# Gate and up of a bilinear GLU as 2x2 blocks with Strassen's seven products, down following per pair of segments

## The chip, the cores and the metric

One core of one Trainium2 chip runs the whole kernel in one launch. The metric is device time in microseconds (us), the median of three runs. The engines are called PE (matrix products), DVE (vector), ACT (scalar functions), POOL (general SIMD) and SP (which only issues DMA transfers here). Each runs its own queue in order and waits on semaphores for the others.

## The reference

A transformer block on x of 2048 rows and 512 columns, modulated by a vector c: attention with a compressive memory over four segments of 512 rows, and then a bilinear gated linear unit.

```python
h = layernorm(x) * (1 + ca) + sa
x = x + ga * A(h)            # 32 heads of 16, 4 segments of 512 rows, each with causal softmax
                             # attention and a memory of the segments before it; then @ wo
h = layernorm(x) * (1 + cb) + sb
x = x + gb * ((h @ w_gate) * (h @ w_up)) @ w_down      # w_gate, w_up: 512 x 1376, w_down: 1376 x 512
```

All is float32. Each large product is made in three matmuls of rounded operands: an operand is split into a rounded high part (`hi`, `H`) and the rest (`lo`, `L`), and high x high, low x high and high x low are summed.

## The kernel before

The four segments of 512 rows (`s`, `L` = 512) go through the attention as 32 units of four heads each, software-pipelined. While PE, DVE, ACT and POOL work on a unit, two generators, `fill_a` and `fill_b`, are advanced step by step to put other work between: `fill_a` the layer norm and the projections of the next segment, `fill_b` the product with wo (`wo_mm`), the layer norm of segment 0 for the GLU (`lnC(0)`) and the preparation of the first two tiles of GLU weights (`prep(0)`, `prep(1)`). Segment 3's product with wo (`ps3`, `wo_row`, `wo_add`) comes after the last unit. Its result rows, x1, go to DRAM (`x1d`).

Then the GLU stage runs by segment. F = 1376 is cut into eleven tiles (`ft`: ten of 128, one of 96; NF = 11). For a tile `i`, `gate_up(i)` makes gate and up (two PSUM banks, 12 matmuls each: 4 blocks of the contraction by 3 parts, each 128 x 128 weights against 512 columns of the transposed, normalised segment `chH`/`chL`). ACT copies the gate out (`gs`), DVE multiplies with up, ACT and DVE split the product (`mH`, `mL`), and 12 matmuls with w_down (`dH`, `dL`) add to four accumulators `acc`, one for each 128 rows. The order is written out:

```python
gate_up(0)
for i in range(NF):
    if i + 1 < NF:
        gate_up(i + 1)
    ...            # 12 matmuls of tile i into acc
```

so that a tile's down stands behind the next tile's gate and up. During segment 0 `prep(i + 1)` brings the weights of the coming tile: gate, up and down by DMA, split by DVE, ACT and POOL, the down rows multiplied by `gbb` (the modulation gb) on DVE. All eleven tiles then stay in SBUF for the other segments. The layer norm of segment s + 1 (`lnC(s + 1)`, a call of `ln`: statistics and normalisation on DVE, 16 transposes on PE in four groups `ctp`, ACT scaling, a split) is made in the middle of segment s. At a segment's end the rows of x1 come back (`xc`), DVE adds `acc`, and the sum is stored.

The program is ordered by a scheduler that keeps each engine's instructions mostly as written and hands out buffers as they come free. Two helpers tie things: `MM` and `TP` chain each PE instruction to the one before, and `pin(i)` orders an instruction behind the last such PE instruction when the schedule is made, without a wait on the chip. `last_pe[0] = None` takes that tie away; the GLU stage before calls `nc.tensor.matmul` itself and is not chained. `btag` is the list of PSUM banks that `bank` takes in turn.

Of the kernel before, what the change touches and what calls it, by code (L numbers as in the profile page):

```python
# [17 lines left out]
P = 128  # L18
# [3 lines left out]
HG = 8  # L22
# [35 lines left out]
def tile_kernel(ctx, tc, x, wq, wk_, wv, wo, beta, w_gate, w_up, w_down, c, w_mod, out):  # L58
# [101 lines left out]
    def ln(pool, hpool, xt, s, sc, sh, pfx, hb, fast):  # L160
# [31 lines left out]
        if first:  # L192
            yield 0.0
        hH, hL = [], []
        for d in range(KT):
            ps = bank(f"{pfx}tp{s}_{d}")
            for t in range(4):
                TP(ps[:, t * P:(t + 1) * P], xt[t][:, d * P:(d + 1) * P], ident)
            h = pool.tile([P, L], F32, tag="hf", name=f"{pfx}hf{s}_{d}", bufs=hb[2])
            A.activation(h, ps, AF.Identity, scale=sc[:, d:d + 1], bias=sh[:, d:d + 1])  # L200
# [143 lines left out]
    def t_step(u):  # L344
# [4 lines left out]
        if jq == 0:  # L349
            orows[ug] = ap.tile([P, 4, HG, DH], F32, tag="orow", name=f"orow{ug}", bufs=2)  # L350
# [22 lines left out]
    def prep(i, pool, rpool, tag, nb):  # L373

        f0, n = ft[i]
        r, raws = {}, {}
        for w, nm in ((w_gate, "g"), (w_up, "u")):
            raws[nm] = raw = rpool.tile([P, KT, P], F32, tag=tag, name=f"cr{nm}{i}", bufs=nb)
            pin(nc.sync.dma_start(raw[:, :, 0:n], w.rearrange("(k p) f -> p k f", p=P)[:, :, f0:f0 + n]))
        rawd = rpool.tile([P, D], F32, tag=tag, name=f"crd{i}", bufs=nb)  # L380
        pin(nc.sync.dma_start(rawd[0:n], w_down[f0:f0 + n, :]))
        yield 0.0
        for nm in "gu":
            raw = raws[nm]
            hi = pool.tile([P, KT, P], F32R, name=f"{nm}H{i}", bufs=1)
            lo = pool.tile([P, KT, P], F32R, name=f"{nm}L{i}", bufs=1)
            pin(vec.tensor_copy(hi[:, :, 0:n], raw[:, :, 0:n]))
            nc.gpsimd.tensor_sub(lo[:, :, 0:n], raw[:, :, 0:n], hi[:, :, 0:n].bitcast(F32))
            r[nm] = (hi, lo)
            yield 0.0  # L390
        hi = pool.tile([P, D], F32R, name=f"dH{i}", bufs=1)
        lo = pool.tile([P, D], F32R, name=f"dL{i}", bufs=1)
        pin(vec.tensor_mul(rawd[0:n], rawd[0:n], gbb[0:n]))
        yield 0.0
        act.activation(hi[0:n], rawd[0:n], AF.Copy)
        nc.gpsimd.tensor_sub(lo[0:n], rawd[0:n], hi[0:n].bitcast(F32))
        r["d"] = (hi, lo)
        wt[i] = r
        yield 0.0
# [633 lines left out]
    for s in range(NSEG):  # L1033
# [30 lines left out]
        for i in range(NF):  # L1064
            if i + 1 < NF:
                gate_up(i + 1)
# [48 lines left out]
```

## Time and profile before

| what | us |
|---|---|
| median of 3 runs (lowest, highest) | 919.63 (918.63, 922.01) |
| span of the profiled execution | 917.9 |
| PE busy in the span | 879.5 |
| attention and its fill, up to the first GLU matmul | 541.4 |
| GLU stage, first to last matmul | 541.4 to 913.2 |

The profiled execution has no time of its own in the listing beside its span; the span is 1.7 us below the median of the runs. A view "by stage" gives, for stretches of the span, each engine's busy time with its number of instructions, the granted clock of PE (1.00 is full), the share of the DMA engines' time and GB/s. A row of a timeline has start and duration in us, the engine, line, operation, output and inputs, and in brackets the idle time before and what ended it. A row of a group has the number of instructions, busy time, mean duration in ns, and the idle time before them.

### The profile page before, as it was taken

The page shows a single profiled execution, that of the slowest core. Times are in us where ns is not written, and L with a number is a line of the kernel's source. Part 1 is how long each engine was busy: PE and PEld are TensorE (multiplying, and loading weights), DVE is VectorE, ACT ScalarE, POOL GpSimd, SP SyncE. Part 2 cuts the span into 40 slices and gives each one's busy share as a digit, 9 for nine tenths or more (in the row PEclk, how much of TensorE's full clock was granted, in tenths as well). Part 3 has the DMA queues.
Part 4 walks back from the last instruction along what each step waited for, and adds up shares of the span by engine and source line. Part 5 has one row for each costly group of instructions (what it writes and reads, how often), then busy time and mean ns, then how long its engine had stood idle before and what let it go on. Part 6 is the DMA issues. An engine that isn't in the chain of part 4 may idle for free.

```text
span 917.9 us, 14194 instructions
## 1 busy us (share of the span) xinstructions
PE 879.5 (96%) x5083; PEld 627.0 (68%) x5084; DVE 531.5 (58%) x1587; ACT 407.7 (44%) x603; POOL 316.1 (34%) x460
## 2 busy tenths in 40 slices
PE   8998999999999899898997999999999999999998
PEld 5765656656656566565655678887888788878886
DVE  8698878887789877687886326552233213321112
ACT  3657767787577765575446402231112111211111
POOL 4445536566465662657324406540000000000000
PEclk8999999999999999998999999999999999999999
DMA  7674544664454544468651343331101110100011
GB/s 226 213 228 135 166 120 157 197 200 145 133 171 166 178 139 127 159 189 285 198 184 55 126 143 104 111 99 50 53 1 46 43 50 0 47 16 31 0 46 46
DMA packets 86215, 109.81 MB, mean 120 GB/s; under 512 B 9504, under 2 KB 58656, under 8 KB 86144
## 3 DMA queue, kind: packets, MB, share of 16 engines
q1 hardware_dynamic: 86000, 108.89, 37.6%
q8 instruction: 40, 0.66, 0.3%
q14 instruction: 31, 0.25, 0.1%
q10 hardware_dynamic: 144, 0.02, 0.0%
HBM read 67.98 MB, written 40.63 MB: 118 GB/s over the span
## 4 chain that ended last, share of the span: by engine, by line
PE 57%; DVE 5%; ACT 2%; DMA 2%; issue 1%; POOL 1%; SPq 1%; DVEq 0%; ACTq 0%
PE gps L1051 13%; PE acc L1072 13%; PE ups L1051 13%; PE wops L85 4%; PE k L85 3%; DVE q L39 3%; PE tb L85 3%; PE q L85 2%; PE qps L85 1%; PE vps L85 1%; ACT pt L313 1%; PE kps L85 1%; PE up L85 1%; PE ctp L88 1%; DMA xr<-in_x_dram 1%
## 5 line engine op out<-in xcount | busy, mean ns | idle before, releaser
L39 DVE CUSTOM_DVE_ANT_0 q<-q,cmask 128x384 f32<-128x384 f32 (+3 forms) x512 | 246.8, 508 | 56.8 <-PE q L85 46.6
L313 ACT ACTIVATE pt<-k 128x1024 f32<-128x1024 f32 x160 | 163.8, 1023 | 76.4 <-PE k L85 74.5
L316 POOL TENSOR_SCALAR_AFFINE_SELECT pt<-pt 128x256 f32<-128x256 f32 (+1 forms) x224 | 99.2, 456 | 168.9 <-ACT pt L313 166.7
L1056 DVE TENSOR_TENSOR gs<-gs,ups 128x512 f32<-128x512 f32 (+1 forms) x44 | 30.2, 687 | 195.1 <-PE ups L1051 195.1
L85 PE MATMUL q<-kst,qst 96*128 96x384 bf16 (+3 forms) x512 | 102.2, 302 | 9.6 <-DVE nm L39 6.8
L85 PE MATMUL k<-qst,kst 98*128 98x384 bf16 (+3 forms) x512 | 98.8, 306 | 6.4 <-ACT pt L313 6.4
L1055 ACT ACTIVATE gs<-gps 128x512 f32<-128x512 f32 (+1 forms) x44 | 26.2, 597 | 146.7 <-PE gps L1051 146.7
L1059 ACT ACTIVATE mH<-gs 128x512 fp32r<-128x512 f32 (+1 forms) x44 | 27.8, 632 | 130.1 <-DVE gs L1056 127.8
L85 PE MATMUL tb<-pt,v 128*32 128x512 f32 (+3 forms) x1024 | 75.9, 436 | 2.5 <-POOL pt L316 2.5
L85 PEld LDWEIGHTS <-kst 98*128 98x128 bf16 x512 | 39.2, 100 | 48.9 <-issue 42.6
L39 DVE DVE_READ_ACCUMULATOR2_ANT nm<- 128x1 f32 x512 | 72.5, 142 | 0.0
L1051 PE MATMUL gps<-chH,gL 128*128 128x512 f32 (+1 forms) x176 | 69.3, 394 | 0.0
L1051 PE MATMUL gps<-chH,gH 128*128 128x512 f32 (+1 forms) x176 | 69.3, 394 | 0.0
L1051 PE MATMUL ups<-chH,uH 128*128 128x512 f32 (+1 forms) x176 | 69.3, 394 | 0.0
L1072 PE MATMUL acc<-dH,mL 128*128 128x512 f32 (+1 forms) x176 | 69.3, 394 | 0.0
L1072 PE MATMUL acc<-dL,mH 128*128 128x512 f32 (+1 forms) x176 | 69.2, 393 | 0.0
L1051 PE MATMUL ups<-chL,uH 128*128 128x512 f32 (+1 forms) x176 | 69.2, 393 | 0.0
L1051 PE MATMUL gps<-chL,gH 128*128 128x512 f32 (+1 forms) x176 | 69.2, 393 | 0.0
L1051 PE MATMUL ups<-chH,uL 128*128 128x512 f32 (+1 forms) x176 | 69.2, 393 | 0.0
L85 PEld LDWEIGHTS <-qst 96*128 96x128 bf16 x512 | 43.8, 98 | 36.5 <-issue 10.5
L1072 PE MATMUL acc<-dH,mH 128*128 128x512 f32 (+1 forms) x176 | 65.0, 395 | 0.0
L85 PEld LDWEIGHTS tb<-pt,v 128*32 128x32 f32 x1024 | 28.6, 109 | 41.4 <-issue 34.9
(215 smaller groups left out, 1664.8 us busy)
## 6 DMA issues: line engine op xcount, KB each, us to landing
kst<-kd SPq DMA_DIRECT2D x32, 384.0 KB, 4.3
qst<-qd SPq DMA_DIRECT2D x32, 384.0 KB, 5.1
wm<-in_w_mod_dram SPq DMA_DIRECT2D x24, 256.0 KB, 5.2
kd<-k SPq DMA_DIRECT2D x16, 384.0 KB, 4.1
qd<-q SPq DMA_DIRECT2D x16, 384.0 KB, 3.2
x<-in_x_dram SPq DMA_DIRECT2D x16, 256.0 KB, 3.8
kd<-k SPq DMA_DIRECT2D x16, 256.0 KB, 3.1
qd<-q SPq DMA_DIRECT2D x16, 256.0 KB, 3.9
```

The source lines that it names most:

```text
L39: i = getattr(self.eng, name)(*a, **k)
L85: return pe(nc.tensor.matmul(*a, **k))
L88: return pe(nc.tensor.transpose(*a))
L313: lpt[0] = act.activation(pt, kp, AF.Exp, scale=0.25)
L316: sels[u, i] = nc.gpsimd.affine_select(w, w, pattern=[[0, w.shape[1]], [1, P]], compare_op=ALU.is_ge, fill=0.0, base=0, channel_multiplier=-1)
L1051: nc.tensor.matmul(ps[0:n], a[:, k, 0:n], b[k], start=j == 0, stop=j == 11)
L1055: act.activation(gs[0:n], pss[0][0:n], AF.Copy)
L1056: vec.tensor_mul(gs[0:n], gs[0:n], pss[1][0:n])
L1059: act.activation(mH[0:n], gs[0:n], AF.Copy)
L1072: nc.tensor.matmul(acc[t], a[0:n, t * P:(t + 1) * P], b[0:n, :], start=i == 0 and j == 0, stop=i == NF - 1 and j == 2)
```

## The change

Segments are taken in pairs (`q` = 0, 1). Gate and up of a pair are one 2x2 block product: the weights are split in four blocks (gate or up, first or second half of the contraction), the transposed rows in four (segment of the pair, half of the contraction), and Strassen's method in Winograd's form makes the four results from seven products of half the contraction, six matmuls each. The block names are `11`, `21`, `22` and the combinations `t1` to `t4`; DVE makes the combinations, ACT and either POOL or DVE split them (`combine`, `parts`). The weights are combined likewise by POOL and split in seven blocks (`prep`), now anew for each pair, three tiles in SBUF at a time. Each tile uses three PSUM banks, two sets in turn; results are summed by DVE from PSUM and from earlier sums.

The products of gate and up (`mid0`, `mid1`, for the pair's two segments) stay in SBUF as float32 for all eleven tiles. Only then does down run, for one segment after the other (`m` = 0, 1): `dprep(f)` loads a tile of w_down (for segment 0 multiplied by `gbb` and also stored to `dwd`; later segments load it from there), splits it and splits the kept product; 12 matmuls follow. During pair 0's down the second pair is prepared: in m = 0 the rows of segments 2 and 3 are normalised (`steps_a`), in m = 1 they are transposed and combined and the first weights prepared (`steps_b`), two steps a tile. All PE instructions of the stage are chained by `MM`.

Segment 1's layer norm moves from the GLU stage into `fill_b`, in place of `prep(1)`, which moves behind the last attention unit. The first pair's `combine` stands between segment 3's wo rows.

```diff
-    def prep(i, pool, rpool, tag, nb):
+    def prep(i, key, pool, nb, rpool, rb):
...
+        w = rpool.tile([P, 8, 2, P], F32, tag="W", name=f"w{key}", bufs=rb)
+        for src, k0, j in ((w_gate, 0, 0), (w_gate, 2, 1), (w_up, 0, 7), (w_up, 2, 2)):
+            pin(nc.sync.dma_start(w[:, j, :, 0:n], src.rearrange("(k p) f -> p k f", p=P)[:, k0:k0 + 2, f0:f0 + n]))
         yield 0.0
...
+        def part(j0, j1, eng):
+            sl = (slice(None), slice(j0, j1), slice(None), slice(0, n))
+            pin(act.activation(hi[sl], w[sl], AF.Copy))
+            eng.tensor_sub(lo[sl], w[sl], hi[sl].bitcast(F32))
+        def comb(o, x, y, op):
+            nc.gpsimd.tensor_tensor(w[:, o, :, 0:n], w[:, x, :, 0:n], w[:, y, :, 0:n], op=op)
+        comb(4, 7, 2, ALU.add)
+        comb(5, 4, 0, ALU.subtract)
+        part(0, 2, nc.gpsimd)
         yield 0.0
+        comb(3, 1, 5, ALU.subtract)
+        comb(6, 0, 7, ALU.subtract)
+        part(4, 6, vec)
+        yield 0.0
+        part(2, 4, nc.gpsimd)
+        yield 0.0
+        part(6, 7, vec)
...
-        pr = prep(1, bc, pb, "cr", 3)
-        next(pr)
         lg = lnC(0, pb, bc, pb, "x1", 4)
...
-        yield from weave(wo_mm(2, us[2], pb), pr, (3, 6, 9, 12))
+        lg = lnC(1, pb, bc, pb, "x1", 4)
+        yield from weave(wo_mm(2, us[2], pb), lg, (0, 1, 2, 3, 4, 5, 6, 7, 8, 9))
+        B["hf"] = yield from lg
...
+    def combine(pr, k, T, b11, b21, b12, b22):
...
+        T["t1", k] = parts(f"t1_{k}_{pr}", t1, nc.gpsimd)
+        sub(t2, b22, t1)
+        T["t2", k] = parts(f"t2_{k}_{pr}", t2, vec)
+        T["22", k] = parts(f"22_{k}_{pr}", b22, nc.gpsimd)
+        sub(t3, b22, b12)
+        T["t3", k] = parts(f"t3_{k}_{pr}", t3, nc.gpsimd)
...
+        T["t4", k] = parts(f"t4_{k}_{pr}", t4, vec)
...
+    PR = {1: (0, "11"), 2: (1, "21"), 3: (3, "22"), 4: (2, "t4"), 5: (4, "t1"), 6: (5, "t2"), 7: (6, "t3")}
+    BK = {1: 0, 2: 0, 5: 1, 3: 1, 6: 2, 7: 2, 4: 2}
+    for q in range(2):
...
+        def product(i, j):
...
+            for k in range(2):
+                bH, bL = T[y, k]
+                for a, b in ((hi, bH), (lo, bH), (hi, bL)):
+                    MM(ps, a[:, x, k, 0:n], b, start=c == 0 and j in (1, 5, 6), stop=c == 5, skip_group_check=True)
+                    c += 1
+            if j == 1:
+                r["p1"] = tmp(f"p1_{q}_{i}")[0:n]
+                act.activation(r["p1"], ps, AF.Copy)
+            elif j == 5:
+                r["p5"] = tmp(f"p5_{q}_{i}")[0:n]
+                act.activation(r["p5"], ps, AF.Copy)
+            elif j == 6:
+                r["u2"] = tmp(f"u2_{q}_{i}")[0:n]
+                vec.tensor_add(r["u2"], ps, r["p1"])
+            elif j == 7:
+                r["u3"] = tmp(f"u3_{q}_{i}")[0:n]
+                vec.tensor_add(r["u3"], ps, r["p1"])
+                vec.tensor_add(r["p5"], r["u3"], r["p5"])
+            elif j == 3:
+                m1 = pc.tile([P, L], F32, tag="mid1", name=f"mid1_{q}_{i}", bufs=NF)
+                vec.tensor_add(r["u2"], ps, r["u2"])
+                mids[i, 1] = m1
+            elif j == 4:
+                m0 = pc.tile([P, L], F32, tag="mid0", name=f"mid0_{q}_{i}", bufs=NF)
+                vec.tensor_add(r["p1"], ps, r["p1"])
+                vec.tensor_mul(m0[0:n], bk[0][0:n], r["p1"])
+                vec.tensor_mul(mids[i, 1][0:n], r["u2"], r["p5"])
...
         for i in range(NF):
+            g = pre.pop(i + 2) if i + 2 < NF else iter(())
...
+            for j in ((2, 5, 6, 3, 7) if q == i == 0 else (6, 5, 2, 7, 3)):
+                product(i, j)
+                next(g, None)
             if i + 1 < NF:
+                begin(i + 1)
+                product(i + 1, 1)
+            product(i, 4)
...
+        for m in range(2):
...
+            def dprep(f):
+                f0, n = ft[f]
+                r = tmp(f"crd{s}_{f}")
+                if s == 0:
+                    pin(nc.sync.dma_start(r[0:n], w_down[f0:f0 + n, :]))
+                    vec.tensor_mul(r[0:n], r[0:n], gbb[0:n])
+                    nc.sync.dma_start(dwd[f][0:n], r[0:n])
+                else:
+                    pin(nc.sync.dma_start(r[0:n], dwd[f][0:n]))
+                dH, dL = tmp(f"dH{s}_{f}", F32R), tmp(f"dL{s}_{f}", F32R)
+                act.activation(dH[0:n], r[0:n], AF.Copy)
+                nc.gpsimd.tensor_sub(dL[0:n], r[0:n], dH[0:n].bitcast(F32))
+                mH, mL = tmp(f"mH{s}_{f}", F32R), tmp(f"mL{s}_{f}", F32R)
+                md = mids.pop((f, m))
+                act.activation(mH[0:n], md[0:n], AF.Copy)
+                vec.tensor_sub(mL[0:n], md[0:n], mH[0:n].bitcast(F32))
+                D0[f] = dH, dL, mH, mL
+            dprep(0)
+            for f in range(NF):
+                if f + 1 < NF:
+                    dprep(f + 1)
...
+                        MM(acc[t], a[0:n, t * P:(t + 1) * P], b[0:n, :],
+                           start=f == 0 and j == 0, stop=f == NF - 1 and j == 2)
+                    if t % 2 == 1:
+                        next(steps, None)
+            for _ in steps:
+                pass
+            for t in range(4):
+                xr = tmp(f"xc{s}_{t}")
+                nc.sync.dma_start(xr, x1d[s][t])
+                vec.tensor_add(xr, xr, acc[t])
+                nc.sync.dma_start(out[rows(s, t), :], xr)
```

In the cut places are the bodies of `steps_a` and `steps_b`, the choice of banks in `begin`, and `ln` divided into `ln_rows` (statistics and normalisation) and `ln_col` (transposes and scaling).

237 lines of the change are left out of this document (154 added, 83 removed).

## The prediction

> **What bounds the kernel now.** I read the page's head first, then the busy time by stage, then the chain of waits in the last stage, then the rows of the engines that the change loads.
>
> ```profile
> span 917.9 us, 14194 instructions
> PE 879.5 (96%) x5083; PEld 627.0 (68%) x5084; DVE 531.5 (58%) x1587; ACT 407.7 (44%) x603; POOL 316.1 (34%) x460
> core 0: us, PE busy (x) PEld busy (x) DVE busy (x) ACT busy (x) POOL busy (x), PEclk, DMA share, GB/s
> 541.40:640.20 98.80, 98.80 (x435) 79.57 (x434) 45.44 (x74) 22.77 (x38) 39.36 (x32) 1.00 0.34 102
> 541.40:913.20 371.80, 371.80 (x1633) 300.03 (x1631) 116.45 (x191) 69.53 (x115) 41.33 (x42) 1.00 0.16 50
> 610.12 2.79 PE gps L1051 x12
> 612.91 2.80 PE ups L1051 x12
> 621.31 2.78 PE acc L1072 x12
> ```
>
> The GLU stage runs from 541.4 to 913.2 us, and PE is busy in all of it at clock 1.00. The chain there is nothing but matmul groups: twelve 512-wide matmuls in 2.79 us, so 0.2325 us each (their mean of 394 ns in the page's groups overlaps with the next). DVE, ACT and POOL are busy 116, 70 and 41 of 372 us: they have room, and POOL has nearly none of its work after 640 us. This stage is set by the number of matmuls. Four segments by eleven F-tiles by 36 matmuls are 132 groups of twelve, 368.3 us; the 3.5 us left are the 12 groups of four transposes of three layer norms, 0.29 us a group.
>
> The profiled execution is known by its span, 917.9 us. The median of the runs is 919.63, 1.7 us more; I carry the sum on the span and add 1.7.
>
> **Removed from PE.** For two segments, gate and up take 48 matmuls a tile; seven products of six take 42. That is 6 fewer in 22 tile-pairs, 132 x 0.2325 = 30.7 us. One layer norm's four transpose groups leave the stage, 4 x 0.29 = 1.2 us. Gain: 31.9 us. Down keeps its count.
>
> **The gate tiles stay on PE.**
>
> ```profile
> L1056 DVE TENSOR_TENSOR gs<-gs,ups 128x512 f32<-128x512 f32 (+1 forms) x44 | 30.2, 687 | 195.1 <-PE ups L1051 195.1
> L1055 ACT ACTIVATE gs<-gps 128x512 f32<-128x512 f32 (+1 forms) x44 | 26.2, 597 | 146.7 <-PE gps L1051 146.7
> L395 ACT ACTIVATE dH<-crd x11: 620/632/635, 448.4 to 622.7; 128x512 fp32r<-128x512 f32 x10, 96x512 fp32r<-96x512 f32 x1
> L396 POOL TENSOR_TENSOR dL<-crd,dH x11: 1271/1295/1678, 449.6 to 623.4; 128x512 fp32r<-128x512 f32 x10, 96x512 fp32r<-96x512 f32 x1
> L388 POOL TENSOR_TENSOR uL<-cru,uH x11: 1007/1296/1741, 444.9 to 619.3; 128x512 fp32r<-128x512 f32 x10, 128x384 fp32r<-128x384 f32 x1
> 553.93 1.67 DVE L1060 TENSOR_TENSOR mL<-gs,mH 128x512 fp32r<-128x512 f32 x1
> 555.52 1.77 DVE L393 TENSOR_TENSOR crd<-crd,gbb 128x512 f32<-128x512 f32 x1
> 553.71 1.35 POOL L388 TENSOR_TENSOR gL<-crg,gH 128x512 fp32r<-128x512 f32 x1 [22.68 <-DVE gH L387]
> 555.01 1.74 POOL L388 TENSOR_TENSOR uL<-cru,uH 128x512 fp32r<-128x512 f32 x1
> 594.52 0.69 DVE L1056 TENSOR_TENSOR gs<-gs,ups 128x512 f32<-128x512 f32 x1 [2.36 <-PE ups L1051]
> 594.53 1.30 POOL L396 TENSOR_TENSOR dL<-crd,dH 128x512 fp32r<-128x512 f32 x1
> ```
>
> The middle four rows are the important ones. A DVE operation with both inputs in SBUF that meets a POOL one takes 1.67 to 1.77 instead of 0.69 us, and POOL's next is stretched to 1.74: from 553.71 to 557.29 the two engines take strict turns, and 3.58 us are two POOL operations of 1.29 and two DVE ones of about 0.5. I call this the turn. With one input in PSUM (594.52, beside POOL's 594.53) nothing is lost.
>
> A gate tile lasts 7 x 6 x 0.2325 = 9.77 us on PE. POOL has two splits of 512 columns (1.29 each) and four combinations of 256; from 1.01 us for 384 and 1.29 for 512 I take 0.77 for one, so 5.7 us. DVE has five operations on PSUM at 0.69 and four on SBUF, 5.9 us; the turn holds 5.7 and about 1.8 us. ACT has two copies of 0.60 and 3.5 splits of 0.63, 3.4 us. All lie below 9.77, each bank is read at least two products (2.8 us) before it is written again, and I cost them at nothing; without that cover the turn's 7.5 us would be bare.
>
> **The first pair's combinations** (sixteen DVE and six POOL operations on SBUF) run while PE does the last wo rows, where DVE is busy 3.74 of 13 us and POOL 1.29:
>
> ```profile
> 528.40:541.40 13.00, 12.09 (x54) 9.54 (x53) 3.74 (x8) 0.60 (x1) 1.29 (x1) 1.00 0.12 41
> 490.00:500.00 10.00, 7.30 (x66) 1.00 0.07 27
> 499.32 0.60 PE L85 MATMUL k<-qst,kst 98*128 98x384 bf16 x4 [1.39 <-ACT pt L313]
> 502.19 0.99 PE L88 MATMUL op<-ident,orl 128*128 128x128 f32 x4 [1.52 <-ACT chf L200]
> 17.39 1.64 PE L85 MATMUL m<-ones,wm 128*128 128x1 f32 x8 [1.75 <-DVE wm L39]
> 17.00:18.00 1.00, 0.61 (x4) 0.84 0.16 57
> 18.00:19.00 1.00, 1.00 (x6) 0.50 0.05 16
> ...
> 24.00:25.00 1.00, 1.00 (x5) 0.75 0.03 8
> ...
> 502.00:503.00 1.00, 0.81 (x5) 0.68 0.19 57
> 503.00:504.00 1.00, 1.00 (x6) 0.50 0.95 330
> 504.00:505.00 1.00, 1.00 (x7) 0.50 0.95 344
> 505.00:506.00 1.00, 1.00 (x8) 0.61 0.85 322
> ```
>
> The order (products 1 and 2 need no combination) gives the rest another 2.8 us: 0, up to 3. Segment 1's layer norm moves into the attention fill, into wo_mm(2). Its model is segment 0's, already there around 490 to 500: PE stood idle 2.7 of 10 us. Its four row loads go to SP there, landing in some 3 us, ahead of their use. Prep 1 leaves the fill, but it was only DVE, POOL and ACT work beside PE. I take +2.7 (0 to 4).
>
> **The seams.** Before, tile i's down is covered by tile i+1's gate and up. Now four stretches of down begin with an empty pipeline.
>
> ```profile
> x<-x1d SPq DMA_DIRECT2D x16, 256.0 KB, 2.7
> DMA to landing us min/median/max: 2.5/3.6/8.4
> L167 DVE BATCH_NORM_STATS2 cst<-x 128x6 f32<-128x512 f32 x12 | 7.6, 679 | 0.0
> L170 DVE BATCH_NORM_AGGREGATE cmv<-cst 128x2 f32<-128x6 f32 x12 | 1.8, 173 | 0.0
> L187 DVE TENSOR_SCALAR x<-x,cmv,cy 128x512 f32<-128x512 f32 x12 | 5.7, 542 | 0.4 <-POOL cy L184 0.4
> 639.04 2.62 SPq L1086 DMA_DIRECT2D out_dram<-xc  x4
> ```
>
> - S1, gate to down of pair 0: behind the last product DVE has two adds or products on PSUM and one on SBUF, then the w_down row times gbb, which the schedule can place only behind the last matmul; four at 0.69 are 2.8 us, then dH on ACT 0.63, then dL on POOL 1.29, needed two matmuls (0.46) after the first: 4.2 us of idle PE (2 if the multiply is placed ahead, 5.3 if it takes 1.77 in the turn); waiting behind that multiply are dH, dL and all of the first down tile. The eight row loads for segments 2 and 3 stand ahead of it on SP, but nothing on SP waits for PE there, so they run ahead.
> - S3, pair 1: no multiply, row, dH and dL can be early, but mL (0.69) stands behind the same three DVE operations (2.1) and is needed one matmul (0.23) after the first: 2.5 us (0 if it is placed ahead).
> - S2 and S4, first to second segment of a pair: the row load is tied behind the last matmul and stands on SP behind the first output stores, which wait for their adds. Landing 2.7 (a row of x1; the second line, 3.6, is that of w_down), dH 0.63, dL 1.29, less the 0.46 of two matmuls: 4.2 us each (2 if the load gets ahead of the stores, 5.1 with a landing of 3.6).
>
> Together 15.1 us, ends 6 and 18.
>
> **First down stretch (segment 0).** PE has 11 x 2.79 = 30.7 us. DVE has 22 operations of 0.69 (multiply and mL), eight statistics of 0.85 and eight normalisations of 0.54, moved here from the fully covered stage: 26.3 us, plus the turn: eleven dL of 1.29 that hold up a DVE operation by half on average, 7.1. That is 33.4, +2.7 us (0 to 7).
>
> **Second down stretch (segment 1).** Here the next pair is made. POOL: 11 dL and 10 splits at 1.29, 27.1, and two tiles' prep at 5.7, together 38.4 us. DVE on SBUF: 11 mL, 8 differences, 4 splits, at 0.49 in the turn, and two preps at 0.8: 12.9. The turn holds 51.3 us. PE has 30.7 and eight transpose groups, 33.0. The second prep (6.5 us) may run on into the next gate tile, which has 2.3 us free; the rest is needed before. Loss 51.3 - 6.5 - 33.0 = 11.8 us; 5.3 if the first prep runs on too, 18.3 if neither does. In the last two segments POOL has 1.29 a tile of 2.79 us: nothing.
>
> **The clock.** The rows from 499 to 506 show a gap of 1.39 us that left the clock alone and one of 1.52 us followed by some 3.5 us at 0.50, which loses 1.75 us of matmuls; the gap of 1.75 us at 17.39 was followed by a drop too. Four seams of 2.5 to 4.2 us can each do that. S2's falls where PE waits for POOL anyway. I take two drops, +3.5 us (0 to 14). [...]
>
> **Sum.** -31.9 + 2.7 + 15.1 + 2.7 + 11.8 + 3.5 = +3.9: a span of 921.8, and with 1.7 a time of 923.5, say 924. The end (four adds, four stores) is unchanged. This case by itself spans 912 to 934: the second stretch's 6.5 us either way and half of what the seams' and the clock's ends leave.
>
> **Rivals.**
> 1. Faster: DVE, ACT and POOL hold work in queues of their own and run ahead of PE. For it: POOL and DVE have room in every gate tile, and nothing but the multiply and the tied loads forces S1, S2, S4. Then seams are at their lower end, 6, the second stretch loses 5.3, the first nothing, no clock drop: -31.9 + 2.7 + 6 + 5.3 = -17.9, time 902. Against it: the turn's 45 us can't shrink by order alone. Chance 0.31, with anything from 900 to 912.
> 2. Slower: in segment 0 the store of the multiplied w_down row stands on SP ahead of the next row's load. Then load (2.7 to 3.6), multiply (0.69, or 1.77 in the turn) and store issue (a quarter of 2.62) make one loop of 4.0 to 6.0 us a tile against 2.79; it decides as soon as the loop is longer than 2.79. Ten tiles at 4.9 lose 21 instead of 2.7: +22, time 942. For it: the store comes before the next load in the program; against: the load is free to go when the tile before begins, about when the store becomes ready. Chance 0.13.
> 3. Clock: all four seams drop, and for the 7 us that the drop at 17.39 lasted (3.5 us each): 14 instead of 3.5, time 934. Chance 0.1.
>
> That products cost more than six matmuls each (a changed matmul rate) has no row for it: same widths, one weight load each; 0.03.
>
> **How the numbers follow.** Forecast 0.43. About 0.5% (4.6 us) is what a measurement can tell from no change, so same is 915.0 to 924.2. Faster: rival 1 and 0.06 of the forecast case's lower edge, 0.37. Same: 0.19, from the forecast case. Slower: the rest of it, 0.18, and rivals 2 and 3 and the last, 0.26: 0.44. A range from 902 to 942 leaves out about 2 in 10, below rival 1's middle and above rival 2's.
>
> **What would show it.** Right: products of six matmuls in 1.40 us with PE at 1.00 through both gate stretches; PE idle 2 to 5 us at four places, ended by ACT dH, POOL dL or DVE mL; in segment 1's down, PE idle some 12 us, ended by POOL dL, while POOL and DVE operations of 1.7 us alternate. Wrong: gaps of PE in the gate tiles; matmul groups off 2.79 us; segment 1's down near 33 us (then rival 1); segment 0's down over 45 us with PE waiting on row loads (rival 2).

## The result, and the profile after

The kernel after took 972.75 us, median of 4 runs (966.29 to 974.16), against 919.42 for the kernel before in the same rounds (4 runs, 918.63 to 922.01). The ratio is 1.0564, 95% interval 1.0526 to 1.0602: slower by 5.6%, outside the range of the prediction.

The head of the page after, and the busy time by stage (columns as in the prediction): last rows of wo, gate tiles of pair 0, down of segments 0 and 1, gate tiles of pair 1, down of segments 2 and 3.

```profile
span 972.5 us, 14734 instructions
PE 882.3 (91%) x4952; PEld 612.0 (63%) x4952; DVE 678.8 (70%) x1723; ACT 480.0 (49%) x748; POOL 483.8 (50%) x619
534.30:554.20 19.90, 15.69 (x54) 12.24 (x53) 16.28 (x17) 6.77 (x12) 16.89 (x12) 0.76 0.13 35
554.20:672.80 118.60, 111.09 (x463) 86.84 (x461) 71.00 (x103) 31.79 (x60) 52.63 (x56) 0.97 0.23 64
676.00:722.90 46.90, 35.94 (x129) 24.71 (x130) 31.02 (x46) 12.31 (x24) 16.25 (x21) 0.96 0.41 132
726.10:783.20 57.10, 43.74 (x164) 32.93 (x165) 37.21 (x27) 29.38 (x51) 47.52 (x36) 0.82 0.34 97
783.20:896.00 112.80, 108.68 (x464) 85.16 (x462) 67.57 (x98) 32.26 (x61) 50.47 (x54) 1.00 0.19 51
896.00:967.80 71.80, 66.44 (x265) 51.89 (x263) 33.58 (x32) 23.27 (x40) 26.16 (x20) 0.93 0.40 115
```

PE has fewer instructions than before (4952 for 5083) but its share fell from 96% to 91%, and in segment 1's down POOL is busy 47.5 of 57.1 us and the granted clock 0.82. The stage of 20 us in the first of these rows had taken 13.00, with DVE at 3.74 and POOL at 1.29. What PE waited for there and behind it (us in total, times, longest):

```profile
PE acc L85 <- DVE mL L1255: 10.4, 12, 1.3
PE gu L85 <- ACT p L1143: 7.5, 11, 0.7
PE acc L85 <- ACT mH L1254: 6.4, 6, 3.3
PE acc1sm L85 <- ACT mH L1254: 6.3, 3, 2.3
PE acc1sm L85 <- DVE mL L1255: 6.1, 5, 3.3
PE gsm L85 <- ACT p L1140: 4.0, 1, 4.0
PE acc1sm L85 <- POOL dL L1251: 3.3, 2, 3.0
```

The groups of the operations that make and split the down tiles and the weights have the turn's price in their means (busy us, mean ns of one): mL on DVE, 1354 ns here, takes 0.69 us alone (its median in the kernel before: 692 ns).

```profile
L1255 DVE TENSOR_TENSOR mL<-mid,mH 128x512 fp32r<-128x512 f32 (+1 forms) x44 | 59.3, 1354 | 58.3 <-ACT mH L1254 57.4
L1251 POOL TENSOR_TENSOR dL<-crd,dH 128x512 fp32r<-128x512 f32 (+1 forms) x44 | 58.7, 1334 | 128.0 <-ACT dH L1250 117.5
L397 POOL TENSOR_TENSOR w<-w 128x256 f32<-128x256 f32 (+1 forms) x88 | 72.5, 833 | 11.3 <-DMA w<-in_w_up_dram 9.7
```

Set against the matmuls alone (0.2325 us each, 0.29 a group of transposes), the stretches account for the whole difference of the spans. The last column is the best kernel found below (e17), in its profiled run, the fastest of its twelve.

| Stretch, us | matmuls alone | predicted loss | after | loss | e17 |
|---|---|---|---|---|---|
| first of segment 3's wo rows at (before: 528.48) | | 2.7 | 534.29 | 5.8 | 529.72 |
| from there to the first gate matmul (before: 13.0) | 13.0 | 0 | 20.0 | 7.0 | 13.0 |
| gate, pair 0 | 107.4 | 0 | 118.5 | 11.1 | 117.9 |
| segment 0's down, with the seams on both sides | 30.7 | 11.1 | 53.4 | 22.7 | 32.8 |
| segment 1's down | 33.0 | 11.8 | 57.1 | 24.1 | 43.5 |
| gate, pair 1 | 107.4 | 0 | 112.7 | 5.3 | 106.9 |
| down of segments 2 and 3, with two seams | 61.4 | 6.7 | 71.9 | 10.5 | 65.8 |

The losses sum to 86.5; less the 31.9 that the matmuls gain this is 54.6, the difference of the spans (972.5 less 917.9). The prediction had 32.3 and 3.5 for the clock.

### The profile page after: what moved, and what is told of

Its sections match the earlier page's. It is cut to its first block, busy times and chain, and to the rows that moved or that the text cites. A ratio compares the mean times of both kernels' runs of the same rounds, so it can differ in the third digit from the quotient of the medians.

```text
span 972.5 us, 14734 instructions
## 1 busy us (share of the span) xinstructions
PE 882.3 (91%) x4952; PEld 612.0 (63%) x4952; DVE 678.8 (70%) x1723; ACT 480.0 (49%) x748; POOL 483.8 (50%) x619
## 4 chain that ended last, share of the span: by engine, by line
PE 63%; DVE 18%; ACT 8%; DMA 4%; issue 3%; POOL 3%; SPq 0%; ACTq 0%; DVEq 0%; POOLq 0%
PE glq L85 8%; PE gu L85 6%; PE tb L85 6%; PE k L85 6%; DVE q L39 6%; PE q L85 5%; PE gb L85 5%; PE vps L85 4%; PE gsm L85 3%; PE qps L85 3%; PE wops L85 3%; PE kps L85 3%; ACT pt L321 2%; DVE mL L1255 2%; PE acc L85 1%
## 5 line engine op out<-in xcount | busy, mean ns | idle before, releaser
L1251 POOL TENSOR_TENSOR dL<-crd,dH 128x512 fp32r<-128x512 f32 (+1 forms) x44 | 58.7, 1334 | 128.0 <-ACT dH L1250 117.5
L1255 DVE TENSOR_TENSOR mL<-mid,mH 128x512 fp32r<-128x512 f32 (+1 forms) x44 | 59.3, 1354 | 58.3 <-ACT mH L1254 57.4
L394 POOL TENSOR_TENSOR AL<-w,AH 128x512 fp32r<-128x512 f32 (+1 forms) x44 | 57.2, 1303 | 72.4 <-ACT AH L393 72.4
L397 POOL TENSOR_TENSOR w<-w 128x256 f32<-128x256 f32 (+1 forms) x88 | 72.5, 833 | 11.3 <-DMA w<-in_w_up_dram 9.7
L1250 ACT ACTIVATE dH<-crd 128x512 fp32r<-128x512 f32 (+1 forms) x44 | 27.6, 628 | 86.3 <-DMA crd<-dwd 34.5
L393 ACT ACTIVATE AH<-w 128x512 fp32r<-128x512 f32 (+2 forms) x88 | 45.9, 562 | 27.4 <-POOL w L397 13.3
L394 DVE TENSOR_TENSOR AL<-w,AH 128x256 fp32r<-128x256 f32 (+3 forms) x41 | 33.4, 832 | 25.8 <-ACT AH L393 25.6
L85 PE MATMUL wops<-woH,oH 128*128 128x512 f32 x64 | 30.4, 475 | 2.9 <-ACT oH L433 1.6
L1254 ACT ACTIVATE mH<-mid 128x512 fp32r<-128x512 f32 (+1 forms) x44 | 27.1, 616 | 8.5 <-DVE p L1150 3.1
L85 PE MATMUL wops<-woH,oL 128*128 128x512 f32 x64 | 27.8, 434 | 2.6 <-DVE oL L39 2.6
```

The lines of the kernel that those rows point to most:

```text
L85: return pe(nc.tensor.matmul(*a, **k))
L393: pin(act.activation(hi[sl], w[sl], AF.Copy))
L394: eng.tensor_sub(lo[sl], w[sl], hi[sl].bitcast(F32))
L397: nc.gpsimd.tensor_tensor(w[:, o, :, 0:n], w[:, x, :, 0:n], w[:, y, :, 0:n], op=op)
L1250: act.activation(dH[0:n], r[0:n], AF.Copy)
L1251: nc.gpsimd.tensor_sub(dL[0:n], r[0:n], dH[0:n].bitcast(F32))
```

## Experiments

A run given with one time alone is one execution. The kernel after lies between 966 and 974 by itself, so these are read by their stretches, in their profiled execution.

**e1 and e2: is segment 0's down the loop on SP?** Rival 2 of the prediction (load, multiply, store, next load) gave 21 us there, and the row loads did come 4.4 us apart.

```diff
-                    nc.sync.dma_start(dwd[f][0:n], r[0:n])
...
+                if s == 0:
+                    nc.scalar.dma_start(dwd[f][0:n], r[0:n])
```

> The store of the multiplied w_down row in segment 0 is issued from ACT's queue, behind dH, instead of SP's. Segment 0's down takes 46.9 us after the change (676.0 to 722.9). Loop theory (the store stands on SP ahead of the next row's load, so that load, multiply and store make one loop of about 4.4 us a tile): the SP loop is gone, two loads are under way at once, and the stretch falls to 31 to 36 us, the whole kernel by 11 to 16 us. Rival (mL waits behind the chain dH, mH on ACT and the turn with POOL's dL, whoever loads): mL is late by the same amount each tile, the stretch stays above 43 us and the kernel gains less than 4 us.

Measured: 971.78; the stretch nearly kept its length (46.6 us from its first matmul to the end of its last, 47.8 before the edit). With the store on ACT's queue the multiply no longer waited for its load (no idle time stands before it in the rows below), and the rhythm stayed. The timeline of e1 on DVE and ACT (start, duration, operation, idle before and its releaser):

```profile
696.30 0.67 DVE L1245 TENSOR_TENSOR crd<-crd,gbb 128x512 f32<-128x512 f32 x1
697.07 0.63 ACT L1249 ACTIVATE dH<-crd 128x512 fp32r<-128x512 f32 x1 [3.13 <-DVE cmv L170]
697.60 0.61 ACT L1255 ACTIVATE mH<-mid 128x512 fp32r<-128x512 f32 x1
697.83 1.27 POOL L1252 TENSOR_TENSOR dL<-crd,dH 128x512 fp32r<-128x512 f32 x1 [3.06 <-ACT dH L1249]
698.32 1.33 DVE L1256 TENSOR_TENSOR mL<-mid,mH 128x512 fp32r<-128x512 f32 x1 [1.26 <-ACT mH L1255]
699.58 1.27 DVE L167 BATCH_NORM_STATS2 cst<-xn 128x6 f32<-128x512 f32 x2
700.85 0.65 DVE L1245 TENSOR_TENSOR crd<-crd,gbb 128x512 f32<-128x512 f32 x1
```

This is another loop of the same length. (The idle time before dH ends with a short statistics operation, cmv, right behind the multiply that dH reads from.) In these rows DVE and ACT take their work strictly in order: multiply, then dH, then mH behind it on ACT, then mL on DVE, 1.33 us beside dL on POOL, then the statistics, and only then the next multiply: 4.5 us. The multiply has no need of mL; it only stands behind it.

In e2 mH and mL are made ahead of the load, dH and dL in every tile:

```diff
+                mH, mL = tmp(f"mH{s}_{f}", F32R), tmp(f"mL{s}_{f}", F32R)
...
                 r = tmp(f"crd{s}_{f}")
```

> In each tile of down the kept product is split (mH on ACT, mL on DVE) ahead of the w_down row (dH on ACT, dL on POOL), in all four stretches. Order theory (mH stands on ACT behind dH, which waits for the row's load, and mL then meets dL in the turn): the waits of PE for mH and mL, 32 us in the four stretches after the change, mostly go or become shorter waits for dH and dL; the kernel gains 10 to 25 us. Loop theory: in segment 0 the row's load is late itself, so the first matmul waits for dH as long as it waited for mH, and only segments 2 and 3 (10.5 us over 61.4) can gain: 3 to 8 us in all.

Measured: 965.74. Segment 0 unchanged: the loop only turns, dH of one tile now stands ahead of mH of the next. Segments 2 and 3, without a multiply, fell from 71.9 to 64.9 us. So the place of mH and mL in the order made most of the loss there: PE's waits fell from 5.3 to 2.6 us, and what the halved clock behind them takes (length times one less the granted clock) from 5.1 to 1.7.

**e5: the multiply out of the loop.** It goes into the gate tiles, one row a tile; segment 0 then loads finished rows.

```diff
+            if q == 0:
+                r = tmp(f"wd{i}")
+                pin(nc.sync.dma_start(r[0:n], w_down[f0:f0 + n, :]))
+                vec.tensor_mul(r[0:n], r[0:n], gbb[0:n])
+                nc.sync.dma_start(dwd[i][0:n], r[0:n])
```

> The multiply of the w_down rows by gbb, its load and its store go into the gate tiles of the first pair, one tile each; down of segment 0 then loads the finished rows as the other three segments do. Segment 0's down takes 46.9 us now, 4.4 us a tile, where PE has 30.7. Order theory: the loop is on DVE and ACT, which take their work strictly in order: multiply 0.68, dH 0.63, mH 0.61, mL 1.34 in the turn with dL, one to two statistics 1.2, next multiply, 4.4 us. Without the multiply nothing on ACT waits for DVE any more, and the stretch falls to 33 to 37 us (segments 2 and 3 have 36 each): the kernel 10 to 14 us faster, less up to 3 in the gate tiles. Rival, the lookahead of one tile (or the turn of mL and dL alone) sets the stretch: it stays at 43 or more.

Measured: segment 0's down 34.9 us instead of 47.8 from its first matmul to the end of its last, PE waiting 1.6 us in it after the first matmul: the order loop is shown. The kernel took 969.58, though: the seam ahead of it grew from 3.3 to 4.9 us, and segment 1's down grew by 6 us, which e7 explains.

**e7: the gate tiles.** PE waits 0.69 us eleven times for the copy of product 5. In odd tiles the first two banks are one double tile, and product 2, into its first half, stood right behind product 5 in its second.

```diff
-            for j in ((2, 5, 6, 3, 7) if q == i == 0 else (6, 5, 2, 7, 3)):
+            for j in ((2, 5, 6, 3, 7) if q == i == 0 else (6, 2, 5, 7, 3)):
```

> Only the order of the products in a gate tile changes: 6, 2, 5, 7, 3 instead of 6, 5, 2, 7, 3. In odd tiles of a pair the first two banks are one double bank, and product 2 waited 0.69 us for ACT's copy of product 5, eleven times. Theory that the double bank counts as one: product 2 then stands ahead of 5 and waits for nothing, product 7 comes right behind 5 in the third bank, and both gate stretches lose 3.4 and 4.1 us, 7.5 in all. Rival: PE is held there by ACT being late, whichever product follows; then the waits move to another product and the gain is under 2 us.

Measured: both gate stretches shorter, 118.5 to 113.1 and 112.8 to 107.7, all eleven waits gone, 10.5 us. Yet the kernel took 968.62: segment 1's down grew from 57.1 to 63.9. The cause is one operation near its end, in e7's timeline:

```profile
772.65 6.00 DVE L1255 TENSOR_TENSOR mL<-mid,mH 96x512 fp32r<-96x512 f32 x1 [6.11 <-ACT mH L1254]
772.31 1.28 POOL L1251 TENSOR_TENSOR dL<-crd,dH 96x512 fp32r<-96x512 f32 x1
773.55 1.42 POOL L397 TENSOR_TENSOR w<-w 128x256 f32<-128x256 f32 x2
774.94 1.26 POOL L394 TENSOR_TENSOR AL<-w,AH 128x512 fp32r<-128x512 f32 x1
776.16 0.71 POOL L397 TENSOR_TENSOR w<-w 128x256 f32<-128x256 f32 x1
776.85 1.25 POOL L394 TENSOR_TENSOR AL<-w,AH 128x512 fp32r<-128x512 f32 x1
778.70 0.80 PE L85 MATMUL acc1sm<-dH,mL 96*128 96x512 f32 x1 [4.01 <-DVE mL L1255]
```

POOL ran six operations of 0.71 to 1.28 us without a gap, and a DVE operation on two SBUF inputs, 0.69 us alone, ended only behind the last of them, 6.00 us after its start. PE waited 4.01 for it, and its matmuls took 0.63 us on both sides of the wait (0.39 at full clock). e5 (6.14) and e16 (6.30) have the same. The kernel after has it too (5.52 us at 778.90), but on a split of weights that nobody waited for. So the edits gained what they should in their own stretches, and this gave more than half of it back.

**e3 and e4: what the two sets of combinations cost.** e3 leaves out the second pair's differences and splits, e4 the first pair's (other blocks stand in their place).

```diff
-                                T2[nm, k] = parts(None, hf[z], nc.gpsimd, hi, lo)
-                        combine(1, k, T2, hf[0], hf[3], hf[1], hf[2])
```

> Leaves out the combining and splitting of the second pair's blocks during segment 1's down (the transposes and the scaling stay; the second pair computes with the first pair's blocks). Segment 1's down takes 57.2 us after the change (726.1 to 783.3). Turn theory (POOL and DVE on SBUF operands take strict turns and their sum sets the stretch): ten POOL operations of 1.29 and twelve DVE ones of 0.49 go, 18.8 us of the turn, and the stretch falls by 15 to 22 us to 35 to 42. Rival (row loads behind other transfers on SP and the clock's drops set it): they stay, and the stretch falls by less than 8 us.

> Leaves out the combining and splitting of the first pair's blocks between the last wo rows (all products use the block 11). From the first of segment 3's wo rows to the first GLU matmul takes 20.0 us after the change against 12.9 before, and the first GLU tile waits another 4.0 us for ACT. Queue theory (oH and oL of the last wo group and the first product's copy stand on ACT and DVE behind the combinations, which wait for each other in the turn; each wait also drops the clock): the wo rows are back to 13 to 14 us, the first tile has no wait, and the kernel gains 10 to 14 us. Rival (the layer norm moved into the attention fill and the weights' preparation hold them up): gain below 5 us.

Measured: e3 961.03, segment 1's down 45.8 us, 11 less: between the two theories, so the combinations are half of that loss. e4 957.91: the first gate matmul comes 12.9 us after the first wo row, as before the change, and the wait of 4.0 for the copy of product 1 shrinks to 0.75. That is 7.1 and 5.6, together 12.7 us, on work that I had costed at nothing (up to 3). PE around the last head group of segment 3 in the kernel after, first, and in e4:

```profile
546.29 0.50 PE L85 MATMUL wops<-woH,oH 128*128 128x512 f32 x1 [1.61 <-ACT oH L433]
549.39 0.79 PE L85 MATMUL wops<-woH,oL 128*128 128x512 f32 x1 [2.60 <-DVE oL L39]
560.00 0.80 PE L85 MATMUL gsm<-chH,AH 128*128 128x512 f32 x1 [4.04 <-ACT p L1140]
```

```profile
541.95 0.49 PE L85 MATMUL wops<-woH,oH 128*128 128x512 f32 x1 [0.69 <-ACT oH L433]
542.68 0.50 PE L85 MATMUL wops<-woH,oL 128*128 128x512 f32 x1 [0.23 <-DVE oL L39]
```

oL and the copy of product 1 were late only because they stood behind differences and splits on DVE and ACT.

**e6: POOL's splits on DVE.** dL and the blocks' low parts.

```diff
-        T["t1", k] = parts(f"t1_{k}_{pr}", t1, nc.gpsimd)
+        T["t1", k] = parts(f"t1_{k}_{pr}", t1, vec)
...
-                nc.gpsimd.tensor_sub(dL[0:n], r[0:n], dH[0:n].bitcast(F32))
+                vec.tensor_sub(dL[0:n], r[0:n], dH[0:n].bitcast(F32))
```

> dL and the low parts of the blocks (t1, t3, 22, 11 and 21) are made on DVE instead of POOL; the combinations of the weights stay on POOL. Turn theory: a DVE operation on two SBUF inputs and a POOL one exclude each other, and POOL needs 1.29 where DVE needs 0.69. Segment 1's down (57.2 us, POOL busy 44 of it) loses 21 POOL operations and gets 21 DVE ones: 44 DVE operations of 0.69 are 30 us, and two preparations on POOL 11: 41 to 46 us, 11 to 16 less. mL goes back from 1.35 to about 0.7. The first pair's stage before the first gate matmul (20.0 us) loses 2 to 4. Rival, order theory: PE waits there for DVE in order behind ACT's splits, and one more operation a tile on DVE makes that longer: segment 1's down within 3 us of 57, segment 0's longer by 3 or more.

Measured: 955.79, the largest gain of one edit. Segment 1's down 46.5 us; in it, 24 more operations on DVE took less time in all than the 27 of the kernel after:

```profile
722.40:769.10 46.70, 40.42 (x165) 30.12 (x166) 35.18 (x51) 29.32 (x53) 20.45 (x16) 0.91 0.40 119
```

27 DVE operations had been busy 37.2 us, 1.38 each; 51 now 35.2, 0.69 each. More work on one engine was cheaper here than the same work shared by two that hold each other up. The first pair's stage did not move (20.0).

**e9: the seams.** The first tile of a down stretch is prepared ahead of the last product, or of the last tile, of what stands before.

```diff
+            else:
+                dprep(0, 0)
             product(i, 4)
...
+                elif m == 0:
+                    dprep(1, 0)
```

> The first tile of each down stretch is prepared one step earlier: ahead of the last product of the last gate tile, and ahead of the last down tile of the segment before. PE's gaps at the four seams are now 3.3, 2.3, 1.9 and 2.3 us, with a clock drop of a few us at some. If the seams are set by where these operations stand in the engines' orders: 6 to 11 us less, gaps under 1 us. Rival: DVE is still busy with the stretch before at that time, and the gap only moves into the next tile: under 3 us less.

Measured: 969.17, in a run whose attention ended 3 us late. PE's gap between gate and down of pair 0 fell from 3.28 to 1.19, the next from 2.34 to under 1, the third from 1.87 to 1.15, the fourth from 1.37 to nothing. At the first and the fourth a wait of 2.0 us stands before the second tile instead, as the rival had it. The stretches are 8 us shorter, as expected of placement.

**e10: the layer norm in the attention fill.**

```diff
-        lg = lnC(1, pb, bc, pb, "x1", 4)
-        yield from weave(wo_mm(2, us[2], pb), lg, (0, 1, 2, 3, 4, 5, 6, 7, 8, 9))
+        yield from wo_mm(2, us[2], pb)
```

> Segment 1's layer norm in the attention fill is left out: copies of segment 0's four high blocks on ACT stand in its place (so the second block row holds other data), everything behind it is unchanged. If this layer norm is what makes the attention's end late, the first of segment 3's rows of wo comes at 528 to 529.5 as in the kernel before (528.48), not at 532 to 537.6 as in the nine runs with it, and the kernel gains 4 to 7 us. Rival: the new order of the pools or of the last loads is what delays it; then the row stays at 532 or later.

Measured: 963.43, and the first of segment 3's wo rows at 528.30, as before the change (528.48). That the layer norm delays the row is shown; by how much is not. With it in place, in the same code up to there, the row comes anywhere from 529.72 (e17) to 537.60 (e9) in the eighteen other profiles, 532.8 in the middle: 1.2 to 9.1 us late, some 4 as a rule.

**e8: the edits of e5, e6, e7 and e9 together**, and e8b without those of e6.

> The four edits together: the multiply of w_down in the gate tiles, low parts of dL and of the blocks on DVE, the product order 6, 2, 5, 7, 3, and the first tile of each down stretch prepared one step early. If the causes are separate, the stretches keep what each edit alone gave: segment 0's down 33 to 35 us (-13), segment 1's 42 to 47 (-10 or more, and no DVE operation of 6 us, since POOL then has no unbroken run of operations there), the gate stretches at 113 and 107.7 (-10.5), the seams at about 1 us (-7), segments 2 and 3 together 64 to 68 (-4 to -8): 972.5 less 44 to 48, a time of 924 to 930. What is left over the forecast's own ideal is then the first pair (12 us), which no edit here touches. Rival, one bound behind all of them (DVE in order): the gains overlap, and the time stays at 938 or more.

> As the run before, but dL and the blocks' low parts stay on POOL. Turn theory: what POOL holds in segment 1's down is not touched, so that stretch stays at 55 to 64 us (the upper end if the last tile's mL again meets POOL's run of five operations and takes 6 us), while segment 0, the seams and the gate stretches gain as above: 938 to 948, 12 to 20 us behind the kernel with the low parts on DVE. Rival, the order alone made segment 1 long: the earlier loads and the missing multiply shorten it to 47 or less, and the two kernels are within 5 us.

Measured: e8 936.56 (4 runs), ratio 1.0173 [1.0135, 1.0210]; e8b 942.09, 1.0227 [1.0190, 1.0265]. The gains overlap: e8 lies between the two expectations. Pair 1's gate tiles (107.8) and segment 0 (34 us) keep their gains. Pair 0's gate tiles do not: 116.7 where e7 had 113.1, since the copy of product 1 now keeps PE waiting 6.36 us instead of 4.29. Nor does segment 1's down: 52.2 us in e8, where e6 alone had 46.5. In e8b it is 56.5, so e6's edit is still worth 5.5 us of the time here, not the 12 or more that was expected. Again one operation, this time on POOL (it takes 0.73 alone, as at 776.44 in the kernel after), while DVE ran splits and differences without a gap:

```profile
732.07 5.01 POOL L397 TENSOR_TENSOR w<-w 128x256 f32<-128x256 f32 x1 [38.58 <-DMA w<-in_w_up_dram]
737.12 0.42 ACT L393 ACTIVATE AH<-w 128x256 fp32r<-128x256 f32 x1 [2.35 <-POOL w L397]
742.58 0.51 PE L85 MATMUL acc1sm<-dH,mH 128*128 128x512 f32 x1 [2.30 <-ACT mH L1174]
```

The splits of weights on ACT waited for POOL, and dH and mH of the next tiles behind them: PE stood 2.30 us for mH.

**e11 to e14: taking the meeting of POOL and DVE away.** On top of e8: e11 puts the first preparation of weights behind product 1 of the first tile, e12 makes the second pair's first two preparations on DVE, e13 does both, and e14 adds the edit of e2.

```diff
+        low = nc.vector if q == 1 and i < 2 else None
+        return prep(i, f"{q}_{i}", (bc, pe_, B.get("pc"))[i % 3], 1, pe_, 2, low)
```

> The four edits together, and the first preparation of weights behind product 1 of the first gate tile instead of among the last rows of wo. The first pair's stage (first wo row to first gate matmul 20.6 us, then a wait of 6.4 us for the copy of product 1) has DVE with some 22 operations on SBUF and POOL with the preparation in the turn. If their meeting makes the stage long, 22 operations of 0.69 are 15.2 us and the loss of 12 us falls to 4 to 6: the kernel 6 to 8 us faster than with the four edits, 929 to 931. Rival, ACT's and DVE's order alone (p1's copy and the last oL behind the splits): less than 3 us, 934 or more.

> The four edits together, and the weights of the second pair's first two tiles, prepared in segment 1's down, combined and split on DVE instead of POOL. Segment 1's down is 52.4 us with the four edits; one combination of 0.73 us on POOL took 5.01 there while DVE had operations without a gap, then ACT's splits of the weights waited for POOL, and dH and mH stood behind them. With no POOL work in the stretch DVE has some 57 operations, about 38 us, and PE 33: if POOL and DVE excluding each other is what is left, the stretch falls to 40 to 45 us and the kernel to 924 to 930. Rival, the order of ACT's and DVE's operations makes it long without any exclusion: 49 us or more.

> Both of the two edits before: if they are separate, their gains add, 916 to 924, about the time of the kernel before; if either turns into a new wait, 927 or more.

> As the run before, with mH and mL made ahead of the row load, dH and dL in each down tile. With the first edit of this kind segments 2 and 3 fell from 71.9 to 64.9 us; with the four edits they stand at 68.5. If mL's place in DVE's order sets them, 64 to 66: 3 to 4 us less than the run before. Rival: with dL on DVE too the order no longer matters; within 1.5 us.

Measured: e11 933.67 (1.0149 [1.0115, 1.0182]), e12 928.41 (1.0097 [1.0065, 1.0129]), e13 927.14 (1.0090 [1.0064, 1.0117]), e14 925.95 (1.0063 [1.0035, 1.0091]). In e12 segment 1's down is 45.8 us, 6.4 less than in e8, with 5.9 us of POOL work left in it; PE's waits in it are now mostly for mL on DVE (4.9 of 7.4 us), and DVE is busy in 38.8 of it:

```profile
703.00:749.00 46.00, 38.56 (x167) 28.80 (x166) 38.83 (x66) 29.37 (x52) 5.92 (x5) 0.96 0.52 152
```

e11 says little on its question: POOL waits for nothing but the load, ran ahead of the place where the code puts it, and met DVE as before (four combinations in 4.27 us from 548.21 on, 4.35 in e8, against 0.73 for one alone), so the stage kept 20 us. e13 is within the noise of e12, and e14 of e13 (7 runs each); segments 2 and 3 did fall from 68.4 to 66.1.

**e15 to e17: the first pair.** In e14 DVE waited eight times 0.7 us for ACT between a difference's high and low part. e15 makes all differences first, the low parts behind; e16 does that alone on the kernel after; e17 is e15 with tile 1's weights loaded only behind the last combination, which holds POOL back.

```diff
+            late.append((eng, lo, f, hi))
...
+        for eng, lo, f, hi in late:
+            eng.tensor_sub(lo, f, hi.bitcast(F32))
```

> As e14, and in the combinations of the blocks all six differences come first on DVE and the low parts after them. In e14 DVE waits eight times 0.7 us for ACT between a difference's high part and its low part, the last oL (which PE waits for 4.06 us) stands behind ten such operations, and the copy of product 1 (5.96 us) stands on ACT behind all splits. Order theory: without these waits DVE's eleven operations ahead of oL end at about 541.5 instead of 545.7, the wait for oL and the clock drop behind it go, the first gate matmul comes 4 to 6 us earlier and the 6 us wait for the copy goes to 0 to 2: 914 to 919, at or below the kernel before. Rival, throughput of DVE in the first pair (22 operations in any order): less than 3 us, 923 or more.

> The same change of order alone on the kernel after, where the low parts of t1, t3 and 22 are on POOL and the first preparation of weights stands among them. If order makes the first pair's loss (12.7 us with the whole combination left out), 5 us or more of it goes; if the meeting of POOL and DVE makes it, under 3 us.

> As e15, and the weights of tile 1 are loaded only behind the last combination of the first pair. In e15 POOL, which waits only for the load, combined the weights at 536.7 to 541.3 and 547.2 to 551.8, and the differences on DVE took 1.1 to 1.7 us there instead of 0.69. Exclusion theory: with POOL away DVE's 23 operations in the first pair end some 5 us earlier, the waits of 3.85 for the copy of product 1 and 2.89 for u shrink to 2 or less together: 3 to 6 us, 915.5 to 918.5, a little under the kernel before. Rival: those waits are ACT's order or tile 1's weights come late: within 1.5 us of e15, or slower.

Measured: e15 921.58 (12 runs, 1.0018 [0.9996, 1.0040]); from the first wo row to the first gate matmul 14.3 us instead of 19.0, the wait for oL 0.27 instead of 4.06; the time lies between the two expectations. e16 972.74: with POOL among them the differences still took their time (wait for oL 3.72), the first pair gained 2.4 us, under the 3 expected of the meeting, and the last mL took 6.30 us. So order alone does little where the two engines meet, and in e11 the place alone did little either. e17 920.38 (12 runs, 1.0008 [0.9989, 1.0027]), 13.0 us to the first gate matmul; what is left stands in the first tiles:

```profile
546.11 0.50 PE L86 MATMUL gsm<-chH,AH 128*128 128x512 f32 x1 [1.87 <-ACT p L1146]
552.72 0.50 PE L86 MATMUL glq<-22_0_0H,AH 128*128 128x512 f32 x1 [2.14 <-ACT p L1149]
557.95 0.50 PE L86 MATMUL glq<-t_0H,AH 128*128 128x512 f32 x1 [3.57 <-DVE u L1152]
```

The last, 3.57, is u queued on DVE behind the first w_down row's multiply, which waits 2.48 for its load: e5's own new wait. The stage is 1.3 us shorter than in e15, but the difference of the times, 1.2 us, is inside the intervals, as the rival had it. No version beat the kernel before; the best two can't be told from it.

## Why the prediction was wrong, step by step

- **Removed from PE, -31.9: right.** Without the waits of 0.69 pair 1's gate tiles take 106.9 to 107.8 us, against 107.4; pair 0's take more (113.1 in e7), for the reason given under the first pair's combinations.
- **The gate tiles, costed at nothing: failed, 10.5 (e7).** The step "each bank is read at least two products before it is written again" took the double tile for two. The eleven waits came of it. The rest of that cover held: pair 1 shows no other wait.
- **The first pair's combinations, 0 (up to 3): failed, 12.7 (e4).** I reckoned DVE's room from its 3.74 busy us in 13, but priced its 16 operations at 0.69, where the rows that I had just quoted show 1.67 to 1.77 beside POOL (in the kernel after the groups of these operations took 0.93 to 1.51 on average), and did not ask who is queued behind them: the last oL, and the copy of product 1.
- **Segment 0's down, 2.7 (0 to 7): failed, about 16.** A sum of busy time (33.4 us) can't see a chain across two engines that each keep their order. Rival 2 had the size (21) and the sign, but the wrong loop: taking away SP's (e1) gave 1 us, taking away the multiply (e5) 13.
- **The turn in segment 1, 11.8 (5.3 to 18.3): the mechanism was right, the term too small, 24.1.** e3 took 11 us away, e6 10.6, and e12, on top of e8, another 6.4. Missing were the waits of dH and mH in ACT's order, the clock of 0.82 (PE busy 43.7 us on 33 us of matmuls), and that the turn is not always one for one; how the 12 us divide among these is open.
- **The seams, 15.1: nearly right.** First tiles waited 3.28 and 0.88, 2.34 and 0.87, 1.87, 1.37 and 0.94: 11.6 us, within the ends given, and set mostly by placement (e9).
- **Segments 2 and 3 beyond their seams, nothing: failed, some 6 us.** That POOL's 1.29 us a tile cost nothing held: behind each segment's first tile PE hardly waits until the last. But of the 10.5 us lost, 4.2 are the first tiles' waits counted above, 1.2 are waits in the last tiles, and 5.1 the halved clock that follows the seams. e2, which makes mH and mL early, cut the waits and with them the clock's loss.
- **The layer norm in the fill, 2.7 (0 to 4): too small as a rule.** 5.8 us in the profile shown, 1.2 to 9.1 over eighteen profiles, some 4 in the middle, against one profile of the kernel before (e10). What makes it vary stays open.
- **The clock, 3.5 (0 to 14), taken as two drops at the seams: failed.** The mean fell from 0.986 to 0.959. By the rows above, length times one less the granted clock is 4.8 us in the first pair's stage, 3.6 in the gate tiles behind it, 1.9 and 10.3 in the downs of segments 0 and 1 and 5.0 in segments 2 and 3, some 25 in all. In the downs of segments 0 and 1 PE waits for others as well, so there not all of it is lost time; in the other stretches, where PE seldom waits behind a drop, most of it is. It lies inside the losses of the other points and is not to be added to them. The drops follow other waits too, not only the four seams: after the first pair's wait of 1.61 us (to 546.29) the clock stood at 0.50 from 547.75 to 554.58, with a wait of 2.60 us (to 549.39) in it and matmuls of 0.63 us. In segment 2 a single wait of 1.87 us (to 898.14) was followed by 3.41 us at 0.50. The last section has more rows on this.

Most of the terms of the sum that failed had one thing in common: they were argued from an engine's free time. The case against rival 1 ("the turn's 45 us can't shrink by order alone") held, and e6 shows why: it shrinks by moving work to the engine that needs 0.69 for it.

## What to carry to other kernels

Before costing added work at nothing, write down its engine's queue at that place and ask what stands behind it; a share of busy time does not answer that, and neither does the order of the code for an engine that waits only for a load. Where two engines hold each other up, as DVE and POOL did here, work can be cheaper on the faster one than shared (in e6 51 operations on DVE took 35.2 us, where 27 had taken 37.2). An edit that gains in its own stretch must be followed to the next: two here gave back 6 us, mostly at one operation. And a wait of PE can cost its clock as well: length times one less the granted clock came to some 25 us here, against 3.5 predicted.

## What the runs showed of the hardware that was not expected

In these runs a DVE operation on two SBUF inputs and a POOL operation held each other up, but not always in strict turns. Where both had several ready they mostly alternated, at 1.7 to 1.8 us each instead of 0.69 and 1.29 (about half of the 128x512 operations in segment 1's down of the kernel after). Four kernels have one DVE operation that waited through a whole run of POOL's (6.00 us in e7, 6.14 in e5, 6.30 in e16, 5.52 in the kernel after), and in e8 a POOL combination of 0.73 us was held for 5.01 while DVE ran without a gap: the waiting side was not always served next. What decides it stays open.

The length of one wait of PE did not tell whether its clock fell. In the kernel after, from 544 us to the last matmul, the clock stood at 0.50 nine times, for 3.41 or 6.83 us. In the 3.41 us ahead of each, PE was idle for 1.68 (930.05:933.46) to 2.92 us (773.03:776.45), all its waits added; in the other 101 pieces of 3.41 us at 1.00, counted on from these, it was idle for 1.46 at most (715.01:718.42). That is one profile from one stage and gives no limit: in its attention 1.31 us of idle PE (489.73:493.14) stood ahead of 0.50 too. So the same wait could cost nothing or 1.7 us: 1.87 us in the kernel after (to 898.14) was followed by 3.41 us at 0.50, while behind the same 1.87 in e1 (to 897.41) and behind 2.85 us in e17 (to 881.35) the matmuls kept 0.39 to 0.50 us. The 3.41 us with the end of the wait and the next on PE (busy time, granted clock), first in the kernel after, then in e1, where 0.68 us of the wait lies ahead of them:

```profile
895.92:899.33 3.41, 1.54 (x7) 1.00 0.32 77
899.33:902.74 3.41, 3.41 (x10) 0.50 0.00 0
```

```profile
896.22:899.63 3.41, 2.22 (x10) 1.00 0.32 77
899.63:903.04 3.41, 3.41 (x17) 1.00 0.29 77
```
